# Second phase of a fused attention and expert kernel: rows turned on VectorE, last tile turned by halves, one layer moved ahead

## The chip, the cores and the metric

The kernel runs on one core of a Trainium2 chip. The metric is the device time of one execution in microseconds (us). Times inside the kernel are those of one profiled execution, counted from its first instruction. TensorE is called PE, its weight loads PEld, VectorE DVE, ScalarE ACT, GpSimd POOL and SyncE SP, as in the profile.

## What is computed

Three stages run one behind the other, all in float32:

```python
kv = einsum('bhsd,bhse->bhde', k, v); out = einsum('bhsd,bhde->bhse', q, kv)   # 8 x 8 heads, 576 x 64
x = out / sqrt(mean(out * out) + 1e-6) * g_norm                                # 4608 tokens of 512
h = x @ w_in; x = (max(h, 0) + alpha * min(h, 0)) @ w_out                      # 512 -> 2048 -> 512
logits = x @ w_gate + modality_bias[modality_id]; e = argmax(logits)           # 8 experts
y = gate * (max(x @ w1[e], 0) @ w2[e])                                         # 512 -> 1024 -> 512
```

## The kernel before, in words

**Precision.** A float32 operand of a large product is split into a high part (hi, cast to the type that PE takes, on ACT) and a remainder (lo, subtracted on DVE or POOL). Each product is then three matmuls: hi by hi, hi by lo, lo by hi.

**First phase.** Twelve chunks of 384 tokens (NCH = 12). For each chunk sixteen steps s: `first(c, s)` makes a block of 128 hidden rows, DVE applies the activation, ACT casts it (ghi, L377), POOL makes glo (L379), and `second(c, s - 1)` adds the block before into three PSUM tiles y (L393). While a chunk runs, the chunk before it gets its eight gate products (`dots`, L410, one per token tile and expert, on DVE), its choice of expert (`choose`, `count` on PE at L456 and L457, `place`) and is scattered by expert into the DRAM buffer `xb`. For the last chunk these follow in the second phase: the copies of y out of PSUM (`y_out`, L404, on ACT), sixteen or fewer of the gate products on DVE, ten on POOL and ACT (`far_mul`, L414, and `far_add`, L419).

**Second phase.** Tiles of 128 rows of `xb`, 41 in any case (MAIN) and up to 43. The experts' weights are loaded into two slots of `W`, each in two halves, by SP (`load_expert`, L593). The expert with most tokens ("leader") is known before the last chunk is through, so tiles 0 to 3 (EARLY = 4) are its rows and start while the last chunk is still being sorted; for later tiles PE reads from a table which slot to use (`words`, L1000).

For each tile i:
- `load_rows(i)`: four DMAs into `xs[:, i % 3]` and one of 8 B per row (`tail`). For tiles 0 to 2 (PLAIN = 3) the pieces are 32 numbers long (128 B), for the others 128 numbers (512 B). SP issues tiles 0 to 5, POOL the rest.
- `turn_rows(i)`: makes the transposed hi and lo in `xhi` and `xlo`, the buffers that hold the chunk's x in the first phase. Tiles 0 to 2: four PE transposes into PSUM (L631), a copy (L643), a subtraction (L644). Later tiles: one DVE transpose of 32 x 32 blocks (L647), a copy that puts the blocks in order (L649), a subtraction (L650).
- `layer1(i)`: 24 matmuls into `pair`, two halves of 512 columns, each with twelve; then the ReLU into `hh`. Tiles 0 to 2 and tile 40: two whole copies on ACT (L687). Others: sixteen quarters of 32 x 256, eight on DVE and eight on ACT, which also move blocks (L692).
- `turn_h(i)`: the transposed hi and lo of `hh` (`hth`, `htl`): with PE transposes (L631, L706, L707) for tiles 0 to 2 and tile 40, else on DVE and ACT (L709, L712, L713), half by half.
- `layer2(i)`: 24 matmuls into one PSUM tile, a scaled copy on ACT (L730), a scatter into the output by POOL (L732).

**Order.** The program order is written out by hand, and every engine works through its own queue in that order. The ends of the first phase and the start of the second are, for PE: `first(11, 15)`, `second(11, 14)`, turn of tile 0's rows, `second(11, 15)`, turn of tile 1's rows, `layer1(0)`, turn of tile 2's rows, the first half of `layer1(1)`, `turn_h(0)`, its second half, `layer2(0)`, the count, `turn_h(1)`, `layer1(2)`, `layer2(1)` with `turn_h(2)` inside, and then the loop (L993): for i = 3 to 40 `turn_rows(i + 1)`, `layer1(i)`, `layer2(i - 1)`, `turn_h(i)`; at last `layer2(40)`. SP's queue at that place is: rows of tile 0, first half of the leader's weights, rows of tiles 1 and 2, second half of the weights (L938 to L942); `layer2(0)` reads the second half.

Of the kernel before, what the change touches and what calls it, by code (L numbers as in the profile page):

```python
# [8 lines left out]
F32 = mybir.dt.float32  # L9
F32R = mybir.dt.float32r  # L10
# [12 lines left out]
D = 512  # L23
# [15 lines left out]
NTAB = 48  # L39
FAR = [(1, e) for e in range(E)] + [(2, 6), (2, 7)]  # L40
PLAIN = 3
EARLY = 4
DOTS = (0, 2, 5, 8, 11, 14, 17, 20, 22, 24)
LAST_DOTS = (0, 3, 6, 9, 12, 15, 18, 21, 24)
# [3 lines left out]
def fused(ctx: ExitStack, tc, qT, kv, g2, wmoe, alpha, wgate, bias, modality, w12, out):  # L48
# [58 lines left out]
    def other(n=512):  # L107
        return (pools[1] if pools else ps_a).tile([128, n], F32, tag="a", name="a")
# [498 lines left out]
    def load_rows(i):  # L607


        if i >= NIT:  # L610
            return
        tab = tab_0[0:1, 1 + i:2 + i] if i < EARLY else tab_row[0:1, i:i + 1]
        q = SP if i < 6 else G
        r = q.value_load(tab, min_val=0, max_val=E * BUCKET + 1024 - 128)
        rows[i] = four(xs[:, i % 3, :])
        src = xb[ds(r, 128)]
        for b in range(4):
            if i < PLAIN:
                to, of = rows[i][:, b].rearrange("p (r i) -> p r i", r=4), src[:, 0:D].rearrange("p (r c i) -> p c r i", r=4, c=4)[:, b]
            else:  # L620
                to, of = rows[i][32 * b:32 * b + 32], src[:, 128 * b:128 * b + 128].rearrange("(a j) c -> j a c", j=32)
            d = q.dma_start(to, of)
        row_dma[:] = [d.ins.name]
        q.dma_start(tail[:, i, :], src[:, D:D + 2])

    order = lambda t: t.rearrange("p (c a j) -> p c a j", c=4, a=4)

    def turned(x, to=None):
        ps = ps_y.tile([128, D], F32, tag="y", name="turned") if pools else to
        for k in range(4):  # L630
            PE.transpose(ps[:, k * 128:(k + 1) * 128], x[:, k * 128:(k + 1) * 128], ident)  # L631
        return ps

    def turn_rows(i):

        x = rows.pop(i)
        o = (i % 3) * 512
        hi = xhi.rearrange("p a b -> p (a b)")[:, o:o + 512]
        lo = xlo.rearrange("p a b -> p (a b)")[:, o:o + 512]
        flat = x.rearrange("p a b -> p (a b)")  # L640
        if i < PLAIN:
            ps = turned(flat, None if pools else spare if i else other())
            A.copy(hi, ps)  # L643
            V.tensor_tensor(lo, ps, hi.bitcast(F32), ALU.subtract)  # L644
            x2[i] = hi, lo
            return
        V.transpose(flat, flat)  # L647
        x = x.rearrange("p a (c j) -> p c a j", c=4)
        A.copy(order(hi), x)  # L649
        V.tensor_tensor(order(lo), x, order(hi).bitcast(F32), ALU.subtract)  # L650
        x2[i] = hi, lo

    def mm(i, ps, a, o, start, stop):
        w = (W if i < EARLY else regs[i][0])[:, o:o + 512]
# [6 lines left out]
    def layer1(i, between=None):  # L661
        if i >= EARLY:
            j, slot = PE.alloc_register(f"j{i}"), PE.alloc_register(f"slot{i}")
            PE.reg_alu(j, words[i // 8], 3 * (i % 8), ALU.logical_shift_right)
            PE.reg_alu(j, j, 7, ALU.bitwise_and)
            PE.reg_alu(slot, j, 1, ALU.bitwise_and)
            PE.reg_alu(slot, slot, SLOT, ALU.mult)
            j, slot = PE.snap(j, min_val=0, max_val=7), PE.snap(slot, min_val=0, max_val=SLOT)
            regs[i] = W[:, ds(slot, SLOT)], j * 2 + 2
            PE.wait_ge(sem_w, j * 2 + 1)  # L670
        hi, lo = x2.pop(i)
        pair = pools[0].tile([128, 2, 512], F32, tag="h", name="h2")
        h = one.tile([128, 2, 512], F32, tag="qT", name="hh")
        for n in range(2):
            ps = pair[:, n, :]
            for k in range(4):
                o = (k * 2 + n) * 1024
                a, b = hi[:, k * 128:(k + 1) * 128], lo[:, k * 128:(k + 1) * 128]
                mm(i, ps, a, o, k == 0, False)
                mm(i, ps, a, o + 512, False, False)  # L680
                mm(i, ps, b, o, False, k == 3)
            if n == 0 and between:
                between()

        plain = i < PLAIN or i == MAIN - 1
        for n in range(2 if plain else 0):
            A.activation(h[:, n].rearrange("p (c b i) -> p b c i", b=4, c=4), pair[:, n].rearrange("p (b c i) -> p b c i", b=4, c=4), AF.Relu)  # L687
        for a in range(0 if plain else 4):
            for b in range(4):
                to, of = h[32 * b:32 * b + 32, :, 128 * a:128 * a + 128], pair[32 * a:32 * a + 32, :, 128 * b:128 * b + 128]  # L690
# [5 lines left out]
        A.sem_inc(sem_1, 1)  # L696
        hh[i] = h

    def turn_h(i):
        h = hh.pop(i)  # L700
        hi = pools[2].tile([128, 2, 512], F32R, tag="kv", name="hth")
        lo = two.tile([128, 2, 512], F32R, tag="raw", name="htl", bufs=3)
        for n in range(2):
            if i < PLAIN or i == MAIN - 1:
                ps = turned(h[:, n])
                A.copy(hi[:, n], ps)  # L706
                V.tensor_tensor(lo[:, n], ps, hi[:, n].bitcast(F32), ALU.subtract)  # L707
                continue
            V.transpose(h[:, n], h[:, n])  # L709
            u, v = order(hi[:, n]), order(lo[:, n])  # L710
            x = h[:, n].rearrange("p (a c j) -> p c a j", c=4, a=4)
            A.copy(u, x)  # L712
            V.tensor_tensor(v, x, u.bitcast(F32), ALU.subtract)  # L713
        ht[i] = (t.rearrange("p n (c t) -> p (n c) t", t=128) for t in (hi, lo))

    def layer2(i, between=None):
        if i >= EARLY:
# [48 lines left out]
    with tc.manual_schedule():  # L766
# [77 lines left out]
        for c in range(NCH):  # L844
# [3 lines left out]
            for s in range(NFB):  # L848
                edge = s == NFB - 1
                between = None  # L850
                if edge and nxt < NCH:
                    between = lambda: [take_x(nxt, k) for k in range(2)]
                elif s == 0 and c > 0:
                    between = lambda: [second(c - 1, NFB - 1, (2,)), y_out(c - 1, 1), y_out(c - 1, 0)]
                if c == 0:
# [21 lines left out]
                if edge and nxt < NCH:  # L877
                    for k in range(2, 4):
                        take_x(nxt, k)
                    second(c, s, (0, 1))  # L880
                elif edge:
                    turn_rows(0)
                    second(c, s)

                if kvb and s in (3, 7):
                    kv_mm(kvb[0], s - 3 and 2)
# [65 lines left out]
        c = NCH - 1  # L952
        y_out(c, 1)
        y_out(c, 2)
        turn_rows(1)
        phase1.close()
        pools.append(ctx.enter_context(tc.tile_pool(name="ps_p", bufs=2, space=PSUM)))
        pools.append(ctx.enter_context(tc.tile_pool(name="ps_o", bufs=1, space=PSUM)))
# [5 lines left out]
        dots(c, 16, 22)  # L964
        layer1(0, lambda: add(0, 1, 2, 3))
        y_out(c, 0)
        turn_rows(2)
        load_rows(3)
        dots(c, 0, 2)
        add(4, 5)  # L970
# [19 lines left out]
        for j in range(1, E):  # L990
            load_expert(j)
        layer2(1, lambda: turn_h(2))
        for i in range(PLAIN, MAIN):  # L993
            if i + 1 < MAIN:
                turn_rows(i + 1)
            layer1(i)
            if i < MAIN - 3:
                load_rows(i + 3)
            if i == PLAIN:
                _, words[:] = nc.values_load_multi_w_load_instructions(  # L1000
                    tab_pe[0:1, 0:6], engines=[PE.engine], min_val=0, max_val=8 ** 8 - 1)
            if i == 8:
                items = nc.values_load(tab_pe[0:1, 6:7], min_val=0, max_val=NIT)
            layer2(i - 1)
            turn_h(i)
        layer2(MAIN - 1)
        with tc.If(items > MAIN):
            for i in range(MAIN, NIT):
# [49 lines left out]
```

## Time and profile before

| | |
|---|---|
| Median of 3 runs | 1359.06 us (1358.51 to 1362.18) |
| Profiled execution | 1360.58 us, its span 1358.9 us, granted PE clock 0.997 |
| PE busy | 1340.9 us (99% of the span) |
| PE weight loads busy | 1155.2 us (85%) |
| DVE, ACT, POOL busy | 987.8, 526.4, 669.5 us (73%, 39%, 49%) |
| DMA | 250.69 MB, 184 GB/s on average |
| Second phase | from `layer1(0)` at 889.93 us to the end |

A row of the timeline gives the start in us, the duration in us, the engine, the line of the program, the operation, the tile written and the tiles read, a count where equal neighbours are merged, and in square brackets how long the engine had been idle and what the profile names as the releaser. An engine's name with a q is its instruction queue, where DMAs are issued and registers loaded. Matmuls overlap in PE's pipeline, so the distance of two starts is the pace, not the duration.

### The profile page before, as it was taken

The numbers are of one execution on the slowest core, as the hardware profiler recorded it, in microseconds if no ns is written. First come the engines' busy times: TensorE is split into PE (matmuls) and PEld (weight loads), VectorE is DVE, ScalarE is ACT, GpSimd is POOL, SyncE is SP. The second block draws the span as 40 slices with busy tenths as digits, with TensorE's granted clock in tenths as the row PEclk, the third lists the DMA queues.
The fourth block names the chain that finished last, engine by engine and source line by source line (L and its number), as shares of the span: only waits on it lengthen the run. The fifth ranks groups of instructions, "written<-read, shape, count | busy, mean of one in ns | idle before, by whom it ended". The sixth has DMA issues, their size and how long they took to land. (4 is left out here: it accounts for less than half of the span.)

```text
span 1358.9 us, 26721 instructions
## 1 busy us (share of the span) xinstructions
PE 1340.9 (99%) x8886; PEld 1155.2 (85%) x8886; DVE 987.8 (73%) x2204; ACT 526.4 (39%) x1147; POOL 669.5 (49%) x643
## 2 busy tenths in 40 slices
PE   8999999999999999999999999999999999999997
PEld 7878888888888988988888988878888888888886
DVE  5778777787877787968787878666766666666662
ACT  3873233332323323232323333144555544445442
POOL 2866555565655564746464656453333333333320
PEclk8999999999999999999999999999999999999999
DMA  7956646453546463546554443557411171637784
GB/s 257 320 191 210 217 145 201 165 200 131 185 163 212 153 221 117 201 160 221 175 191 171 140 164 117 184 204 243 177 48 48 58 281 47 269 106 298 305 322 162
DMA packets 88949, 250.69 MB, mean 184 GB/s; under 512 B 19245, under 2 KB 39213, under 8 KB 86640
## 3 DMA queue, kind: packets, MB, share of 16 engines
q1 hardware_dynamic: 77056, 220.82, 46.2%
q0 software_dynamic: 11760, 28.14, 6.3%
q8 instruction: 78, 1.28, 0.4%
q14 instruction: 55, 0.45, 0.1%
HBM read 158.69 MB, written 91.54 MB: 184 GB/s over the span
## 5 line engine op out<-in xcount | busy, mean ns | idle before, releaser
L365 PE MATMUL h<-xhi,W 128*128 128x384 f32 x1536 | 429.7, 341 | 0.5 <-POOL W L183 0.2
L379 POOL TENSOR_TENSOR glo<-gg,ghi 128x384 fp32r<-128x384 f32 x192 | 234.7, 1223 | 340.1 <-ACT ghi L377 324.4
L393 PE MATMUL y<-W,ghi 128*128 128x512 f32 x1152 | 299.1, 394 | 4.8 <-ACT ghi L377 3.7
L377 ACT CAST ghi<-gg 128x384 fp32r<-128x384 f32 x192 | 98.8, 515 | 501.1 <-DVE gg L373 232.6
L365 PEld LDWEIGHTS h<-xhi,W 128*128 128x128 f32 x1536 | 280.4, 188 | 11.2 <-ACT xhi L354 1.2
L365 PE MATMUL h<-xlo,W 128*128 128x384 f32 x768 | 257.9, 336 | 0.0
L393 PEld LDWEIGHTS y<-W,ghi 128*128 128x128 f32 x1152 | 213.0, 188 | 44.6 <-ACT ghi L377 8.7
L410 DVE CUSTOM_DVE_ANT_0 junk<-yrow,wg_sb 128x512 f32<-128x512 f32 x242 | 221.0, 913 | 8.7 <-ACT yrow L404 3.1
L655 PE MATMUL h<-W,xhi 128*128 (+1 forms) x656 | 206.5, 396 | 0.0
L655 PE MATMUL y<-W,hth 128*128 (+1 forms) x656 | 204.6, 393 | 1.9 <-DVE lg L410 1.5
L213 POOL TENSOR_TENSOR raw<-raw 128x512 f32<-128x512 f32 x128 | 203.3, 1588 | 0.0
L372 DVE TENSOR_SCALAR gg<-h,alpha_sb 128x384 f32<-128x384 f32 x176 | 108.2, 615 | 106.3 <-PE h L365 104.2
L732 POOL DMA_INDIRECT out_dram<-kvbd,tail x41 | 43.2, 1054 | 282.8 <-ACT kvbd L730 239.6
L393 PE MATMUL y<-W,glo 128*128 128x512 f32 x576 | 163.4, 392 | 0.0
L365 PEld LDWEIGHTS h<-xlo,W 128*128 128x128 f32 x768 | 144.3, 188 | 6.0 <-DVE xlo L355 0.2
L655 PEld LDWEIGHTS h<-W,xhi 128*128 128x128 f32 x656 | 122.6, 187 | 29.9 <-ACT xhi L649 0.3
L655 PEld LDWEIGHTS y<-W,hth 128*128 128x128 f32 x656 | 123.0, 188 | 28.9 <-DVE lg L410 1.9
L655 PE MATMUL h<-W,xlo 128*128 (+1 forms) x328 | 129.4, 394 | 0.0
L393 PEld LDWEIGHTS y<-W,glo 128*128 128x128 f32 x576 | 107.9, 188 | 23.4 <-POOL glo L379 0.8
L655 PE MATMUL y<-W,htl 128*128 (+1 forms) x328 | 127.8, 390 | 0.0
L692 DVE TENSOR_SCALAR hh<-h 32x256 f32<-32x256 f32 x296 | 123.2, 416 | 4.6
L713 DVE TENSOR_TENSOR htl<-hh,hth 128x512 fp32r<-128x512 f32 x74 | 51.2, 692 | 99.0 <-ACT hth L712 97.6
(221 smaller groups left out, 1482.1 us busy)
## 6 DMA issues: line engine op xcount, KB each, us to landing
wsp<-raw SPq DMA_DIRECT2D x128, 512.0 KB
W<-wsp SPq DMA_DIRECT2D x16, 4096.0 KB
raw<-in_w_dram SPq DMA_DIRECT2D x128, 256.0 KB
kvt<-in_kv_dram SPq DMA_DIRECT2D x30, 512.0 KB
xs<-xb POOLq DMA_DIRECT2D x140, 64.0 KB
raw<-in_wmoe_dram SPq DMA_DIRECT2D x17, 511.8 KB
qT<-in_qT_dram SPq DMA_DIRECT2D x11, 768.0 KB
wg_sb<-in_wmoe_dram SPq DMA_DIRECT2D x15, 511.8 KB
```

What stands on the lines that cost most here:

```text
L213: G.tensor_tensor(lo, lo, hi, ALU.subtract)
L365: PE.matmul(ps, w_at(fb, part)[:, k * 128:(k + 1) * 128], x[:, k, :], start=(i == 0), stop=(i == 11))
L372: V.tensor_scalar(gg, ps, 0.0, alpha_sb[:, fb:fb + 1], ALU.min, ALU.mult)
L377: A.copy(ghi, gg)
L379: G.tensor_tensor(glo, gg, ghi.bitcast(F32), ALU.subtract)
L393: PE.matmul(y_t[c][t], a[:, t * 128:(t + 1) * 128], w, start=(fb == i == 0), stop=(fb == NFB - 1 and i == 2))
L410: V.tensor_tensor_reduce(spare if i >= 22 else junk, y, wg_sb[:, e, :], 1.0, 0.0, ALU.mult, ALU.add, lg_t[c][:, t, e:e + 1])
L655: m = PE.matmul(ps, a, w, start=start, stop=stop)
L692: m = V.tensor_scalar(to, of, 0.0, None, ALU.max) if mine else A.activation(to, of, AF.Relu)
L713: V.tensor_tensor(v, x, u.bitcast(F32), ALU.subtract)
L732: d = G.indirect_dma_start(out=out, out_offset=IndirectOffsetOnAxis(ap=tail[:, i, 1:2].bitcast(I32), axis=0), in_=y, in_offset=None, bound ...
```

## The change

- Tiles 0 to 2: their rows are loaded in the 512 B pieces, and turned like those of the later tiles, with a DVE transpose. The steps are written into the last two steps of the first phase: the DVE transpose of tile 0 at the end of step 14, its hi inside `first(11, 15)`, its lo and all of tiles 1 and 2 in step 15, ahead of `second(11, 15)` in the program and of the copies `y_out(11, 1)` and `y_out(11, 2)`.
- Tiles 3 and 40 (SPLIT): the ReLU is done per half of `pair` in quarters of 32 x 128. The first half's quarters, its transpose and its hi are written between the two halves of `layer1`, the rest behind it; tile 40 is no longer turned on PE.
- `layer2(3)` comes directly behind `layer2(2)`, ahead of `layer1(4)`; `turn_rows(4)` is written inside it, and the table's words are loaded behind it. From tile 4 on the loop is as before, with `layer2(4)` behind `layer1(5)`.

```diff
+SPLIT = (PLAIN, MAIN - 1)
 ...
         for b in range(4):
-            if i < PLAIN:
-                to, of = rows[i][:, b].rearrange("p (r i) -> p r i", r=4), src[:, 0:D].rearrange("p (r c i) -> p c r i", r=4, c=4)[:, b]
-            else:
-                to, of = rows[i][32 * b:32 * b + 32], src[:, 128 * b:128 * b + 128].rearrange("(a j) c -> j a c", j=32)
-            d = q.dma_start(to, of)
+            d = q.dma_start(rows[i][32 * b:32 * b + 32], src[:, 128 * b:128 * b + 128].rearrange("(a j) c -> j a c", j=32))
...
+    def turn_blocks(i):
+        flat = rows[i].rearrange("p a b -> p (a b)")
+        V.transpose(flat, flat)
+
+    def take_rows(i, part):
+        hi, lo = (order(t.rearrange("p a b -> p (a b)")[:, (i % 3) * 512:(i % 3) * 512 + 512]) for t in (xhi, xlo))
+        x = rows[i].rearrange("p a (c j) -> p c a j", c=4)
+        if part == 0:
+            A.copy(hi, x)
+            return
+        V.tensor_tensor(lo, x, hi.bitcast(F32), ALU.subtract)
+        rows.pop(i)
...
     def turn_rows(i):
...
-        if i < PLAIN:
-            ps = turned(flat, None if pools else spare if i else other())
-            A.copy(hi, ps)
-            V.tensor_tensor(lo, ps, hi.bitcast(F32), ALU.subtract)
-            x2[i] = hi, lo
-            return
...
+        turn_blocks(i)
+        take_rows(i, 0)
+        take_rows(i, 1)
...
             if n == 0 and between:
                 between()
-
-        plain = i < PLAIN or i == MAIN - 1
+            if n == 0 and i in SPLIT:
+                quarters(i, pair, h, slice(0, 1))
+                half_hi(i, h, 0)
+
+        plain = i < PLAIN
...
+        if not plain:
+            quarters(i, pair, h, slice(i in SPLIT, 2))
+        A.sem_inc(sem_1, 1)
+        hh[i] = h
+        if i in SPLIT:
+            half_lo(i, h, 0)
+            half_hi(i, h, 1)
+            half_lo(i, h, 1)
+            parts(i)
...
+                elif edge:
+                    between = lambda: take_rows(0, 0)
...
                 elif edge:
-                    turn_rows(0)
+                    take_rows(0, 1)
+                    turn_blocks(1)
+                    take_rows(1, 0)
+                    turn_blocks(2)
+                    take_rows(2, 0)
+                    take_rows(1, 1)
+                    take_rows(2, 1)
                     second(c, s)
+
+                if nxt == NCH and s == NFB - 2:
+                    turn_blocks(0)
...
-        turn_rows(1)
...
-        turn_rows(2)
...
         layer2(1, lambda: turn_h(2))
-        for i in range(PLAIN, MAIN):
+        layer1(3)
+        load_rows(6)
+        layer2(2)
+        layer2(3, lambda: turn_rows(4))
+        _, words[:] = nc.values_load_multi_w_load_instructions(
+            tab_pe[0:1, 0:6], engines=[PE.engine], min_val=0, max_val=8 ** 8 - 1)
+        for i in range(EARLY, MAIN):
...
-            layer2(i - 1)
-            turn_h(i)
+            if i > EARLY:
+                layer2(i - 1)
+            if i not in SPLIT:
+                turn_h(i)
         layer2(MAIN - 1)
```

`quarters`, `half_hi`, `half_lo` and `parts` hold the operations that stood in `layer1` and `turn_h` before, for one half: sixteen quarters; a DVE transpose and an ACT copy; a DVE subtraction.

## Rows read from the trace of the kernel before

**Rows 1.** Part 1 of the page: busy time, share of the span, instructions.
```profile
PE 1340.9 (99%) x8886; PEld 1155.2 (85%) x8886; DVE 987.8 (73%) x2204; ACT 526.4 (39%) x1147; POOL 669.5 (49%) x643
```

**Rows 2.** Timeline of PE from 886 to 910 us, in part.
```profile
887.06 0.60 PE L631 MATMUL a<-ident,xs 128*128 128x128 f32 x4
887.41 1.64 PE L393 MATMUL y<-W,ghi 128*128 128x512 f32 x6
...
902.27 0.39 PE L655 MATMUL h<-W,xlo 128*128 128x512 f32 x1
904.18 0.71 PE L655 MATMUL y<-W,hth 128*128 128x512 f32 x2 [1.52 <-DVE lg L410]
...
909.77 0.19 PE L456 MATMUL a<-hb,tri 128*128 128x24 bf16 x1
```

**Rows 3.** Timeline of SP's queue: DMA issues, from tile 1's rows on.
```profile
875.37 9.18 SPq L622 DMA_DIRECT2D xs<-xb  x4
...
888.46 2.07 SPq L622 DMA_DIRECT2D xs<-xb  x4
...
891.93 0.35 SPq L593 DMA_DIRECT2D W<-wsp  x1
...
928.18 1.95 SPq L622 DMA_DIRECT2D xs<-xb  x4
```

**Rows 4.** DMA view of 874.2 to 886, 884.8 to 886 and 904.5 to 910 us.
```profile
DMA packets 669, 4.27 MB, mean 362 GB/s; under 512 B 540, under 2 KB 540, under 8 KB 540
...
DMA packets 358, 0.11 MB, mean 91 GB/s; under 512 B 356, under 2 KB 356, under 8 KB 356
...
q1 hardware_dynamic: 720, 0.26, 22.6%
```

**Rows 5.** Timeline of ACT, POOL and DVE from 886 to 907 us, in part.
```profile
886.58 0.51 ACT L377 CAST ghi<-gg 128x384 fp32r<-128x384 f32 x1 [3.65 <-DVE gg L373]
889.55 1.07 ACT L404 COPY yrow<-y 128x512 f32<-128x512 f32 x2 [1.27 <-PE y L393]
890.21 7.60 POOL L414 TENSOR_TENSOR kvbd<-yrow,wg_sb 128x512 f32<-128x512 f32 x6 [2.03 <-ACT yrow L404]
895.98 1.06 ACT L687 ACTIVATE hh<-h 128x512 f32<-128x512 f32 x2
899.46 1.08 ACT L706 CAST hth<-turned 128x512 fp32r<-128x512 f32 x2 [0.22 <-PE turned L631]
907.04 0.18 DVE L437 CAST hb<-hot 128x24 bf16<-128x24 f32 x1
```

**Rows 6.** One line's instructions: durations in ns (least, median, most).
```profile
L712 ACT CAST hth<-hh x74: 607/619/622, 938.7 to 1336.4; 128x512 fp32r<-128x512 f32 x74
L692 DVE TENSOR_SCALAR hh<-h x296: 404/416/421, 934.4 to 1331.7; 32x256 f32<-32x256 f32 x148
```

**Rows 7.** Timeline of PE and DVE from 922 to 940 us, in part.
```profile
922.71 0.63 PE L655 MATMUL h<-W,xhi 128*128 128x512 f32 x2
...
928.30 0.62 PE L655 MATMUL y<-W,hth 128*128 128x512 f32 x2
...
932.42 0.71 DVE L647 STREAM_TRANSPOSE xs<-xs 128x512 f32<-128x512 f32 x1 [7.35 <-DMA xs<-xb]
...
933.84 0.73 PE L655 MATMUL h<-W,xhi 128*128 x2
...
939.80 0.62 PE L655 MATMUL y<-W,hth 128*128 128x512 f32 x2
```

**Rows 8.** Line 1000: the load of the table's words on PE's sequencer.
```profile
L1000 PEldq TENSOR_LOAD <-tab_pe x1: 1018/1018/1018, 924.1 to 924.1; - x1
```

**Rows 9.** Timeline of DVE and PE from 1337 us on, in part.
```profile
1337.02 0.69 DVE L713 TENSOR_TENSOR htl<-hh,hth 128x512 fp32r<-128x512 f32 x1 [0.69 <-ACT hth L712]
...
1344.68 1.03 PE L631 MATMUL turned<-ident,hh 128*128 128x128 f32 x8
...
1351.75 0.40 PE L655 MATMUL y<-W,htl 128*128 x1
```

More of the change, by code (lines that the diff above doesn't have):

```diff
@@ L626, in fused, with turned @@
     order = lambda t: t.rearrange("p (c a j) -> p c a j", c=4, a=4)
-    def turned(x, to=None):
-        ps = ps_y.tile([128, D], F32, tag="y", name="turned") if pools else to
+    def turned(x):
+        ps = ps_y.tile([128, D], F32, tag="y", name="turned")
         for k in range(4):
@@ L632, in turned @@
         return ps
-    def turn_rows(i):
[L636 to L640, printed above, removed]
-        if i < PLAIN:
-            ps = turned(flat, None if pools else spare if i else other())
-            A.copy(hi, ps)
-            V.tensor_tensor(lo, ps, hi.bitcast(F32), ALU.subtract)
-            x2[i] = hi, lo
-            return
[L647 to L651, printed above, removed]
+    def turn_blocks(i):
[9 more added lines that the diff above has]
+        rows.pop(i)
+        x2[i] = (t.rearrange("p a b -> p (a b)")[:, (i % 3) * 512:(i % 3) * 512 + 512] for t in (xhi, xlo))
+    def turn_rows(i):
+        turn_blocks(i)
+        take_rows(i, 0)
+        take_rows(i, 1)
     def mm(i, ps, a, o, start, stop):
@@ L683, in layer1, with quarters @@
                 between()
-        plain = i < PLAIN or i == MAIN - 1
+            if n == 0 and i in SPLIT:
+                quarters(i, pair, h, slice(0, 1))
+                half_hi(i, h, 0)
+        plain = i < PLAIN
         for n in range(2 if plain else 0):
             A.activation(h[:, n].rearrange("p (c b i) -> p b c i", b=4, c=4), pair[:, n].rearrange("p (b c i) -> p b c i", b=4, c=4), AF.Relu)
-        for a in range(0 if plain else 4):
+        if not plain:
[7 more added lines that the diff above has]
+            parts(i)
+    def quarters(i, pair, h, ns):
+        for a in range(4):
             for b in range(4):
-                to, of = h[32 * b:32 * b + 32, :, 128 * a:128 * a + 128], pair[32 * a:32 * a + 32, :, 128 * b:128 * b + 128]
+                to, of = h[32 * b:32 * b + 32, ns, 128 * a:128 * a + 128], pair[32 * a:32 * a + 32, ns, 128 * b:128 * b + 128]
                 mine = a < 2
@@ L695, in layer1, with halves, half_hi, half_lo @@
                 tc.add_to_no_dep_group(f"quarters{mine}", m.ins)
-        A.sem_inc(sem_1, 1)
-        hh[i] = h
+    def halves(i):
+        if i not in ht:
+            ht[i] = (pools[2].tile([128, 2, 512], F32R, tag="kv", name="hth"),
+                     two.tile([128, 2, 512], F32R, tag="raw", name="htl", bufs=3))
+        return ht[i]
+    def half_hi(i, h, n):
+        hi, _ = halves(i)
+        if i < PLAIN:
+            of = turned(h[:, n])
+            A.copy(hi[:, n], of)
+            return of
+        V.transpose(h[:, n], h[:, n])
+        A.copy(order(hi[:, n]), h[:, n].rearrange("p (a c j) -> p c a j", c=4, a=4))
+    def half_lo(i, h, n, of=None):
+        hi, lo = halves(i)
+        if i < PLAIN:
+            V.tensor_tensor(lo[:, n], of, hi[:, n].bitcast(F32), ALU.subtract)
+            return
+        V.tensor_tensor(order(lo[:, n]), h[:, n].rearrange("p (a c j) -> p c a j", c=4, a=4), order(hi[:, n]).bitcast(F32), ALU.subtract)
+    def parts(i):
+        ht[i] = tuple(t.rearrange("p n (c t) -> p (n c) t", t=128) for t in halves(i))
     def turn_h(i):
         h = hh.pop(i)
-        hi = pools[2].tile([128, 2, 512], F32R, tag="kv", name="hth")
-        lo = two.tile([128, 2, 512], F32R, tag="raw", name="htl", bufs=3)
         for n in range(2):
[L704 to L714, printed above, removed]
+            half_lo(i, h, n, half_hi(i, h, n))
+        parts(i)
     def layer2(i, between=None):
@@ L998, in fused @@
                 load_rows(i + 3)
-            if i == PLAIN:
-                _, words[:] = nc.values_load_multi_w_load_instructions(
-                    tab_pe[0:1, 0:6], engines=[PE.engine], min_val=0, max_val=8 ** 8 - 1)
             if i == 8:
                 items = nc.values_load(tab_pe[0:1, 6:7], min_val=0, max_val=NIT)
-            layer2(i - 1)
-            turn_h(i)
+            if i > EARLY:
+                layer2(i - 1)
+            if i not in SPLIT:
+                turn_h(i)
         layer2(MAIN - 1)
```

## The prediction

> **What bounds the kernel now.** First the page: TensorE (PE) is busy for 99% of the span [rows 1], so only three things can pay: PE work that goes away, gaps in PE's row, and what ends those gaps. Then PE's row in the timeline, read for gaps between 885 us and the end. I number the second phase's tiles from 0; "hi" and "lo" are the two parts into which an operand is split, "turn" is the transpose. There are four places. (a) Three groups of four PE transposes turn the rows of tiles 0 to 2; one group stands here, the other two are alike [rows 2]. (b) The first matmul of layer2(0) starts at 904.18; the one before it started at 902.27 and the pitch is 0.23, so PE stands 1.68 us [rows 2]. The profile names a dot product of VectorE, but layer2(0) reads none of those; I read it as the second half of the leader's weights, issued at 891.93 [rows 3], which it does read. (c) Layer1(4) waits for the rows of tile 4, which VectorE turns when they land, at 932.42 [rows 7]. (d) At the end the eight transposes of tile 40 and the copies behind them stand alone between layer2(39) and layer2(40) [rows 9]. The rest of the second phase is one matmul per 0.23 us without a gap.
>
> **Part 1, rows of tiles 0 to 2 on VectorE.** Away go 3 x 4 PE transposes. Each group moves PE's next work by 887.41 - 887.06 = 0.35 us [rows 2], and the matmuls behind it lose another 0.07 to 0.1 in refilling (the first six take 1.64 where steady ones take 1.54), so 0.43 x 3 = 1.3 us. Against it: the last MoE product now follows at once on the one before it, at 887.06, and its operand ghi is written at 886.58 + 0.51 = 887.09 [rows 5]; its weight load, due 0.22 ahead, slips to about 887.15, which costs 0.2. PE gains 1.1 us by layer2(0).
>
> By the Trainium skill's page "TensorE: Matmul & The Clock Gate" (Part 4: PE-mode transpose) a transpose takes about 275 ns in a kernel's context; at that price the twelve here and the eight at the end would give 5.5 us. The rows show why that price does not add up: four last 0.60 together [rows 2], so they overlap, and the sum above goes by what follows them.
>
> The loads of these rows change too: the same four DMAs each, but in pieces of 512 B instead of 128 B, a quarter as many. On SP's queue they stand between the two halves of the leader's weights, order unchanged. Before, the four of tile 1 took 9.18 us to issue behind the first half, so tile 2's were issued only at 888.46 and the second half at 891.93 [rows 3]; layer2(0) could start 904.18 - 891.93 = 12.25 after that. After, I expect SP not to be held back, and all of them to lie in the queue when the first half ends. When is that? Its 129 large packets (669 less 540 small ones) go out within 874.2 to 886.0, eight on each of 16 engines, so about 1.3 us a packet, and only two start after 884.8 [rows 4]: most engines are through at some 885.9, the slowest near 887.2. A tile in 512 B pieces, its tail and semaphores take 22.6% of 5.5 us = 1.24 per engine (tile 3's) [rows 4]; two tiles 2.5. From landing to VectorE I put 0.5, at most 1.1 (tile 4 was turned at 932.42, 2.3 after its last issue ended, against 1.24 of data [rows 3, 7]). So tile 2 can be turned at **R** = 888.9 (engines alike) to 890.8 (the slowest, late landing); 0.3 less if SP gets through tile 0 sooner too. I take 889.5, between the two engine cases with the short landing (888.9 and 890.2). The second half then follows from 888.3 to 889.7 on instead of 892.2, and lands near 900 to 901.4. PE wants it at 902.5 - 1.1 = 901.4: the 1.68 goes, with at most 0.2 left.
>
> What is late next is the choice of experts for the last chunk. The count matmul, at 909.77 [rows 2], needs VectorE's hb, which is ready at 907.22 [rows 5]: 2.5 us of cover. By PE alone it would move to 909.77 - 1.1 - 1.68 = 907.0. But ACT and VectorE now wait for R ahead of the last chunk's work. On ACT tile 2's hi stands before the copies of y (L404). From R: turn 0.71 [rows 7], hi 0.62 [rows 6], so those copies start at R + 1.4 (before 889.55). First product on POOL 0.66 later, relu(0) behind four sums another 895.98 - 890.21 = 5.77 later, the copies of tile 0's turned h 2.8 after that (before 899.46 - 895.98 = 3.48, less 0.48 for tile 2's hi, now done, and 0.2 of waiting for PE), hb 907.22 - 899.46 = 7.76 later [rows 5]. Sum: R + 18.4. VectorE's own queue (turn, two lo, eight dot products) is ready sooner. So the count starts at the later of 907.0 and R + 18.4; with R = 889.5 at 907.9. **The head gains 909.77 - 907.9 = 1.9 us**; ends: R = 888.6 gives 2.8, R = 890.8 gives 0.6. From the count on (places, scatter, table, rows 3 to 5, with SP's and POOL's queues behind them) everything follows the count and shifts with it.
>
> Tile 0's turn lies on VectorE between the last two activations, where it waits for PE, and its hi on ACT before ghi, after the matmuls that read the old xhi: nothing.
>
> **Part 2, layer2(3) ahead of layer1(4).** The PE work is the same. Layer1(4) starts 5.5 us later, so the wait for tile 4's rows goes: layer1(4) took 939.80 - 933.84 = 6.0 where layer1(3) took 928.30 - 922.71 = 5.6 [rows 7], a gain of **0.4**. Layer2(3) wants tile 3 5.5 us after layer1(3). By halves: eight VectorE operations of 32x128 per half. Their price is not in the trace: 32x256 takes 0.42 [rows 6], 512 columns 0.69 [rows 9], so 1.08 ns a column and 0.28 for 128; the bounds are half of 0.42 and the whole. At 0.28 x 8 = 2.3 a half, first-half lo is ready 2 us early, at the upper bound just in time: nothing. Layer2(4) now follows layer1(5) directly, so tile 4 has 5.6 us for quarters (8 x 0.42 = 3.4), turn (0.7), hi (0.6) and lo (0.7) = 5.4 plus 0.3 of start; lo is wanted by the third matmul: a wait of 0.05, at most 0.2. The table's words are now loaded on PE's sequencer directly before their use: a load of 1.02 at 924.1 [rows 8] and register steps behind it, begun 4.2 us before the matmul that stood next in the order, at 928.30 [rows 7]; with that lead I cost it at nothing, at most 0.5. POOL's load of tile 7's rows moves behind one more output scatter; the rows are wanted two tiles later: nothing.
>
> **Part 3, tile 40 by halves.** Layer2(40) starts where the transposes did, at 1344.68 [rows 9]. At the pitch of layer2(2), 5.5 us for 24 matmuls [rows 7], its last one starts 5.27 later, at 1349.95 instead of 1351.75 [rows 9]: **1.8 us**. Cover: VectorE is free at 1337.02 + 0.69 = 1337.71 [rows 9]; quarters 2.3, turn 0.7, quarters 2.3, lo 0.7 end at 1343.7 where 1345.1 will do; turn, hi and lo of the second half at 1345.8 where 1347.4 will do. At 0.42 a quarter the first lo comes at 1346.0: 0.9 of the gain would go.
>
> **Sum.** 1.9 + 0.4 - 0.05 + 1.8 = 4.05 us. The profiled execution took 1360.58 (span 1358.9 and 1.7 around it), 1.5 over the median of the runs, 1359.06; the gaps are no part of that difference that I can see, so I take the sum off the median: **1355.0 us**.
>
> **Rivals.** *Tile 2 late as before.* SP is still held behind the weights, and tile 2 is issued near 888.5 and there at 892.1. Speaks for it: the four issues of tile 1 that were held (9.18) [rows 3], with nothing in the trace that shows 512 B pieces behind weights. Against: a quarter of the pieces. Then count at 910.5, the head loses 0.7, the sum is 1.4 or a little less: 1357.8. *R early.* No slow engine, R at 888.6 or below, PE itself sets the count: 2.8 + 2.15 = 4.95: 1354.1. *PE waits for the first halves.* Tiles 3 and 40 now read one half of the pair in PSUM while PE writes the other. If that held PE until the first half's quarters are done, tile 3 would cost 2.5, tile 40 (VectorE free at 1337.71, the half done at 1344.68 - 5.5 - 2.8 = 1336.4) 3.6, together 6.1: 1361.1, slower. It turns slower where the two waits pass 4.05. No operation of the trace reads one half beside writes into the other; against it speaks that the halves are separate 512-column regions. The Trainium skill's page "PSUM — Partial Sum Buffer" (PSUM bank collisions raise a hardware error) wants readers and TensorE on different banks, and counts 512 FP32 values to a bank; no run here shows it.
>
> **How the numbers follow.** Forecast 0.45, R early 0.18, tile 2 late 0.25, PE waits 0.05, something unseen 0.07. Range: from 1353.7 (R early, less the spread of the median) to 1358.3 (tile 2 late, with a bit of part 3 lost). A measurement of this kernel tells about 0.3%, 4.1 us, from no change: below 1355.0 is faster. The forecast sits on that line: half of it and most of R early make 0.38 for faster; 0.58 within; 0.04 slower.
>
> **What would show it.** Right: no transposes of xs on PE; layer2(0) without a gap; SP's five issues of tile 1 in about 2.5 us; ACT's copies of y at 890 to 891.5 and the count right behind hb; layer1(4) without a gap; layer2(40) straight behind layer2(39). Wrong: tile 2's DMAs still issued after 888, relu(0) or hb later than here with PE waiting for them, or a gap of PE between the halves of layer1(3) and layer1(40).

## The result, and the profile after

The changed kernel takes **1366.57 us** (median of six executions, 1363.32 to 1369.89); the kernel before took 1359.13 beside it. The ratio is 1.0051, interval 1.0033 to 1.0069: about 7 us slower, where the prediction said 4 us faster. The page of one execution of 1363.32 us (span 1361.7), part 1, which answers to [rows 1]:

```profile
PE 1337.8 (98%) x8866; PEld 1152.0 (85%) x8866; DVE 996.6 (73%) x2233; ACT 531.5 (39%) x1169; POOL 669.6 (49%) x643
```

PE has 20 instructions less (the transposes), is busy for 3 us less, and yet the span is longer: the time has gone into PE's gaps. The view of what PE waits for, from 880 us to the end, is short (engine and line, what it waited for, us in total, times, longest):

```profile
PE h L652 <- DVE hh L703: 6.3, 2, 3.8
PE turned L628 <- ACT hh L687: 1.5, 1, 1.5
PE y L652 <- DMA W<-wsp: 0.2, 1, 0.2
```

Lines are those of the changed kernel: L652 the matmuls of both layers, L703 the quarters, L687 the relu of tiles 0 to 2, L628 the turn of h on PE, L394 the last MoE products, L457 the count, L438 hb, L619 the loads of rows, L594 those of weights, L633 the turn of rows on VectorE, L639 and L641 their hi and lo, L720 and L721 the turn and the hi of h, L405 the copies of y, L415 POOL's products, L753 the scaling of a result. In the kernels of the experiments lines behind L652 can stand up to four further down. PE's timeline in part (start, duration, engine, line, operation; in brackets the idle time before it and its releaser), with VectorE's first quarters of tile 3; it answers to [rows 2, 7, 9]:

```profile
882.32 1.54 PE L394 MATMUL y<-W,ghi 128*128 128x512 f32 x6
...
896.68 1.15 PE L628 MATMUL turned<-ident,hh 128*128 128x128 f32 x8 [1.49 <-ACT hh L687]
...
900.86 0.71 PE L652 MATMUL y<-W,hth 128*128 128x512 f32 x2 [0.23 <-DMA W<-wsp]
906.53 0.17 PE L457 MATMUL a<-hb,tri 128*128 128x24 bf16 x1
...
919.46 0.63 PE L652 MATMUL h<-W,xhi 128*128 128x512 f32 x2
...
922.03 0.39 PE L652 MATMUL h<-W,xlo 128*128 128x512 f32 x1
922.45 2.36 DVE L703 TENSOR_SCALAR hh<-h 32x128 f32<-32x128 f32 x8 [0.29 <-PE h L652]
924.96 0.70 PE L652 MATMUL h<-W,xhi 128*128 128x512 f32 x2 [2.54 <-DVE hh L703]
...
927.81 0.62 PE L652 MATMUL y<-W,hth 128*128 128x512 f32 x2
...
955.50 0.63 PE L652 MATMUL h<-W,xhi 128*128 x2
...
1335.24 0.39 PE L652 MATMUL h<-W,xlo 128*128 x1
1339.40 0.79 PE L652 MATMUL h<-W,xhi 128*128 x2 [3.77 <-DVE hh L703]
...
1340.42 1.05 PE L652 MATMUL h<-W,xhi 128*128 x2
...
1343.81 0.63 PE L652 MATMUL y<-W,hth 128*128 x2
...
1354.58 0.40 PE L652 MATMUL y<-W,htl 128*128 x1
```

Layer1(3) and layer1(40) stop in the middle: twelve matmuls into the first half of the pair, then nothing until the first half's quarters have been read, then twelve into the second. Behind tile 40's stop the matmuls are also slow: two take 1.05 where two took 0.63. The page gives the granted clock of such a stretch (stretch, its length, PE's busy time and instructions, granted clock in the fourth number, DMA share, GB/s), after first, then before:

```profile
10.00:15.00 5.00, 4.61 (x34) 1.00 1.08 355
...
1340.00:1345.00 5.00, 5.00 (x17) 0.67 0.11 43
```
```profile
5.00:10.00 5.00, 2.64 (x15) 0.90 0.80 236
10.00:15.00 5.00, 5.00 (x22) 0.50 1.10 334
15.00:20.00 5.00, 5.00 (x36) 0.92 1.02 388
```

So for part of 1340 to 1345 PE ran at 1.2 GHz, the lower level. The second fence warns of something else: the profiled execution of before spent some 7 us of its startup at the lower level, that of after did not; the first MoE matmul starts at 27.10 before and at 24.31 after, and the last MoE product but one, ahead of all that the change touches on PE, at 884.99 and 882.32, 2.67 earlier. Of the twelve profiled executions of this study six have a granted clock of 0.66 or less from 10 to 15 us and four one of 0.67 to 0.76 near 100 us (one of them both), whatever the kernel. Absolute times of two profiles can't be subtracted here; distances from a common mark in PE's row can. Three marks of before that are not shown yet:

```profile
884.99 1.54 PE L393 MATMUL y<-W,ghi 128*128 128x512 f32 x6
...
956.42 0.63 PE L655 MATMUL h<-W,xhi 128*128 x2
...
1339.18 0.62 PE L655 MATMUL y<-W,hth 128*128 x2
```

| from ... to (us) | before | after | change | forecast |
|---|---|---|---|---|
| last MoE product but one ... count | 24.78 | 24.21 | -0.57 | -1.9 |
| count ... layer1(3) | 12.94 | 12.93 | -0.01 | 0 |
| layer1(3) ... layer1(6) | 33.71 | 36.04 | +2.33 | -0.35 |
| layer1(6) ... last matmul | 395.33 | 399.08 | +3.75 | -1.8 |
| **all** | 466.76 | 472.26 | **+5.5** | -4.05 |

The third line holds tile 3's stop, 2.76 (2.70 of standing, from 922.03 + 0.23 to 924.96, and 0.06 of slower first matmuls behind it), less 0.43 by which layer1(4), now without a gap, is shorter. The fourth holds tile 40's stop (1335.24 + 0.23 to 1339.40, 3.93), the slow matmuls behind it (twelve in 4.41 where twelve took 2.8, 1.6) and the gain of the tail, 1.80: layer2(39) to the last matmul takes 10.77 where it took 12.57.

### The profile page after: what moved, and what is told of

It is laid out like the page before. It is cut to its first block, busy times and chain, and to the rows that moved or that the text cites. A ratio compares the mean times of both kernels' runs of the same rounds, so it can differ in the third digit from the quotient of the medians.

```text
span 1361.7 us, 26738 instructions
## 1 busy us (share of the span) xinstructions
PE 1337.8 (98%) x8866; PEld 1152.0 (85%) x8866; DVE 996.6 (73%) x2233; ACT 531.5 (39%) x1169; POOL 669.6 (49%) x643
## 5 line engine op out<-in xcount | busy, mean ns | idle before, releaser
L394 PE MATMUL y<-W,ghi 128*128 128x512 f32 x1152 | 299.1, 394 | 4.8 <-ACT ghi L378 3.8
L394 PEld LDWEIGHTS y<-W,ghi 128*128 128x128 f32 x1152 | 213.0, 188 | 44.9 <-ACT ghi L378 9.3
L652 PE MATMUL h<-W,xhi 128*128 (+1 forms) x656 | 207.5, 397 | 6.3 <-DVE hh L703 6.3
L652 PE MATMUL y<-W,hth 128*128 (+1 forms) x656 | 204.4, 393 | 0.2 <-DMA W<-wsp 0.2
L394 PE MATMUL y<-W,glo 128*128 128x512 f32 x576 | 163.4, 392 | 0.0
L652 PEld LDWEIGHTS h<-W,xhi 128*128 128x128 f32 x656 | 123.5, 189 | 37.2 <-ACT hh L703 7.1
L652 PEld LDWEIGHTS y<-W,hth 128*128 128x128 f32 x656 | 123.1, 188 | 27.1 <-DVE htl L726 0.6
L703 DVE TENSOR_SCALAR hh<-h 32x256 f32<-32x256 f32 (+1 forms) x320 | 129.0, 403 | 15.2 <-PE h L652 10.3
L652 PE MATMUL h<-W,xlo 128*128 (+1 forms) x328 | 129.9, 396 | 0.0
L703 ACT ACTIVATE hh<-h 32x256 f32<-32x256 f32 (+1 forms) x320 | 117.3, 367 | 30.5 <-PE h L652 26.4
L394 PEld LDWEIGHTS y<-W,glo 128*128 128x128 f32 x576 | 107.9, 188 | 23.5 <-POOL glo L380 0.8
L652 PE MATMUL y<-W,htl 128*128 (+1 forms) x328 | 127.7, 389 | 0.0
```

The lines of the kernel that those rows point to most:

```text
L652: m = PE.matmul(ps, a, w, start=start, stop=stop)
```

## The experiments

Theory: PE's stop is a wait written into the program, because the pair of halves is guarded as one piece; it costs the two gaps and, where the clock falls behind them, more. The rivals: reading one bank beside writing its neighbour is slow in itself; the halves were needed, and what lost was something else; the loss sits in the head.

**The wait taken away.** The two tiles' second-half matmuls are told apart from the first half's quarters; nothing else changes.

```diff
+                free = n == 1 and i in SPLIT
-                mm(i, ps, a, o, k == 0, False)
+                mm(i, ps, a, o, k == 0, False, free)
...
+        if free:
+            for mine in (True, False):
+                tc.declare_no_dep(m.ins, group=f"quarters{mine}", reason="they read the other bank of the pair")
```

> The changed kernel, but the second-half matmuls of layer1(3) and layer1(40) are no longer made to wait for the quarters that read the first half of the pair. My theory: PE's two stops are a wait written into the program for those quarters, and neither the data nor the memory needs it. Then both gaps (2.76 and 3.93 us) go, the half-clock stretch behind the second (about 1.6) with them, and what is left against the kernel before is the gain of the head 0.57, of layer1(4) 0.43 and of the tail 1.80: together 2.8 us faster, about 1356.3, ratio 0.998. Rival A: ACT and VectorE reading one bank while PE writes its neighbour slow each other, so that the time is lost anyway as slower matmuls or quarters: 2 to 6 us slower than before. Rival B: the loss is not in these gaps but in the head (tile 2's rows late): then it stays at 1.005.

Measured: **1357.33 us**, ratio 0.9983 (0.9974 to 0.9992). PE and VectorE in the middle of layer1(3), and the marks at the end:

```profile
924.28 0.40 PE L652 MATMUL h<-W,xlo 128*128 128x512 f32 x1
924.52 0.63 PE L652 MATMUL h<-W,xhi 128*128 128x512 f32 x2
...
924.72 2.37 DVE L707 TENSOR_SCALAR hh<-h 32x128 f32<-32x128 f32 x8 [0.56 <-PE h L652]
...
1337.78 0.62 PE L652 MATMUL y<-W,hth 128*128 x2
...
1348.54 0.39 PE L652 MATMUL y<-W,htl 128*128 x1
```

PE goes from one half to the next at its pitch of 0.23 while VectorE reads the first half, and the eight quarters take 2.37 as they did with PE standing (2.36): neither slows the other, and rival A is out. From mark to mark the changes against before are -0.33, +0.01, -0.42 and -1.80, together 2.5; the medians say 2.35. The theory holds, and the stretches of parts 2 and 3 are shorter by what the prediction gave them. The Trainium skill's page "PSUM — Partial Sum Buffer" (PSUM bank collisions raise a hardware error) asks for a guard bank by bank, and a half is one bank; the trace agrees that more is not needed.

**Tiles 3 and 40 in one piece.** No halves, so nothing to guard.

```diff
-SPLIT = (PLAIN, MAIN - 1)
+SPLIT = ()
...
         layer1(3)
+        turn_h(3)
```

> The changed kernel, but tiles 3 and 40 are turned on VectorE in one piece, behind both halves, as the other tiles are: no first half is read before the second is written, so no wait inside layer1. Quarters of 32x256 (8 x 0.42 = 3.4 us), turn 0.7, hi 0.6, lo 0.7 give 5.4 against the 5.5 us of a layer2. Theory (only the wait inside layer1 costs): both gaps are gone, at most 0.3 us is waited before layer2(3) and layer2(40): 2.3 to 2.8 us faster than before, 1356.5, ratio 0.998. Rival (the halves are needed because a whole tile is too late behind one layer2): more than 1 us lost before layer2(3) and again before layer2(40), so no faster than before.

Measured: 1359.42, ratio 0.9999 (0.9990 to 1.0008). That is the rival's time, but not for its reason: both stops are gone, and layer2(3) starts without a gap although its tile, too, has only the 5.5 us of one layer2 to be turned in; only layer2(40) is late. ACT's row and PE's in this kernel:

```profile
1344.49 0.69 ACT L753 ACTIVATE kvbd<-y,tail 128x512 f32<-128x512 f32 x1 [2.40 <-PE y L652]
1345.07 0.61 ACT L721 CAST hth<-hh 128x512 fp32r<-128x512 f32 x1
...
1345.73 0.74 PE L652 MATMUL y<-W,hth 128*128 x2 [1.28 <-ACT hth L721]
```

Tile 40's hi stands in ACT's queue behind the scaling of layer2(39)'s result, which waits for PE; its turned block was ready at 1343.24. So the order is at fault, not the length. From layer2(39) on this kernel takes 12.58, 1.8 more than without PE's wait, and ahead of layer1(4) another 0.44 goes, behind a gap of 0.22; together 2.3, where the ratios say 2.2. Its profiled execution also has a granted clock of 0.87 and 0.78 from 895 to 905 us, behind a wait of 1.82 ahead of the turn of tile 0's h, and with it a head of 25.51 us, 0.73 longer than before.

**The same, turned ahead of layer2(39).**

```diff
+            if i == MAIN - 1:
+                turn_h(i)
             if i > EARLY:
                 layer2(i - 1)
-            if i not in SPLIT:
+            if i < MAIN - 1:
                 turn_h(i)
```

> e2_whole (tiles 3 and 40 turned in one piece), and the turning of tile 40 is written ahead of layer2(39). In e2_whole PE waited 1.28 us before layer2(40), and ACT's row shows why: tile 40's hi stands behind the scaling of layer2(39)'s result, which waits for PE until 1344.49, while the turned block lay ready from 1343.24. Theory: with the order changed hi starts at 1343.2, hi and lo of the first half are there by 1344.5, PE waits at most 0.3 us instead of 1.28, and the kernel is 1.0 to 1.4 us faster than e2_whole against the same kernel before: ratio 0.9990 or a little less. So not the halves but their order in ACT's queue is what part 3 needs. Rival (the whole tile is simply too late behind 5.5 us of layer2): 0.9999 as e2_whole.

Measured: 1358.46, ratio 0.9989 (0.9980 to 0.9998). ACT in this kernel:

```profile
1344.08 0.62 ACT L721 CAST hth<-hh 128x512 fp32r<-128x512 f32 x1 [1.19 <-DVE hh L720]
...
1346.72 0.69 ACT L753 ACTIVATE kvbd<-y,tail 128x512 f32<-128x512 f32 x1
```

Hi now starts when the turned block is there, PE shows no gap ahead of layer2(40), and layer2(39) to the last matmul takes 10.79, as with the halves. By the ratios 1.4 us comes back; the two intervals just overlap, so it is the rows that show it. Part 3's gain needs no halves, so no wait: only that ACT's queue takes the turn before the scaling.

**Part 1 alone.** The changed kernel with tile 40 and the order of the layers put back as they were.

```diff
-SPLIT = (PLAIN, MAIN - 1)
+SPLIT = ()
...
-        plain = i < PLAIN
+        plain = i < PLAIN or i == MAIN - 1
...
-        layer1(3)
-        load_rows(6)
-        layer2(2)
-        layer2(3, lambda: turn_rows(4))
...
-        for i in range(EARLY, MAIN):
+        for i in range(PLAIN, MAIN):
```

> Part 1 alone: the rows of tiles 0 to 2 turned on VectorE, the order of layers 1 and 2 and the turning of tile 40 as before. Theory (from the profile of the changed kernel): SP is held at tile 2's rows, the copies of y stand on ACT behind tile 2's hi, and the count comes 0.57 us earlier than before: 0.6 faster, 1358.5, ratio 0.9996. My prediction on record said 1.9 (ratio 0.9986). Rival (the loss of the whole change sits in part 1, which only starts 2.7 us early by chance in the one profile): slower than before by 2 us or more.

Measured: 1358.63, ratio 0.9990 (0.9981 to 0.9999). From the mark to the count its profile has 24.16, 0.62 less than before. The head gains a third of its forecast and loses nothing. The same profile holds one thing more. VectorE turns tile 4's rows in it at

```profile
930.95 0.71 DVE L633 STREAM_TRANSPOSE xs<-xs 128x512 f32<-128x512 f32 x1 [5.46 <-DMA xs<-xb]
```

which is 45.25 us behind the mark (885.70) where it was 47.43 before (932.42 from 884.99 [rows 7]), and layer1(4) takes 5.59 where it took 5.96, though the layers stand in their old order. So part 1 alone already brings the 0.4 that was forecast for part 2.

**Without part 3.** Tile 40 turned on PE, tile 3 still by halves.

```diff
-SPLIT = (PLAIN, MAIN - 1)
+SPLIT = (PLAIN,)
...
-        plain = i < PLAIN
+        plain = i < PLAIN or i == MAIN - 1
```

> The changed kernel without part 3: tile 40 is turned on PE as before, tile 3 still by halves with PE's wait inside layer1(3). Theory: of the gaps only tile 3's 2.76 us stays: 2.76 - 0.57 - 0.43 = 1.8 us slower than before, 1360.8, ratio 1.0013. If the granted clock also falls behind tile 3's gap, another 1 to 3 us, and the matmuls behind that gap stand at twice the pitch. Rival (part 3 is no loss, all of it is tile 3 and the head): as slow as the changed kernel, 1.005.

Measured: 1363.20, ratio 1.0027 (1.0015 to 1.0038): 3.5 us slower. Its profile has tile 3's stop alone ([2.54], and 36.06 from layer1(3) to layer1(6)) and the full clock behind it: 2.35 more there, 0.39 less in the head, 2.0 together, as the theory has it. The other 1.5 I put down to the clock of other executions: three of the seven had a mean granted clock of 0.993 or 0.994, the median one 0.997, against 0.998 here. That is inferred, since only their mean clock is known; the next run shows such a stretch.

**The changed kernel once more.**

> The changed kernel unaltered, one more profiled execution. Six executions of it fall into two groups, mean granted clock 0.997 (1363.3 to 1365.7 us) and 0.993 (1367.4 to 1369.9). Theory: the granted clock falls for some microseconds behind PE's waits, always behind tile 40's 3.8 us and sometimes behind one of the shorter ones (1.5 us ahead of the turn of tile 0's h, 2.5 us inside layer1(3)); an execution of the second group shows a stretch at half clock behind one of these as well, some 3.7 us more. Rival: the second group is slow somewhere in the first phase, away from the change. In an execution of the first group only the stretch behind tile 40's gap shows.

Measured: one execution, 1368.67 us. PE inside layer1(3), and the granted clock of the stretches around it:

```profile
928.91 1.19 PE L652 MATMUL h<-W,xhi 128*128 128x512 f32 x2 [2.54 <-DVE hh L703]
...
930.33 1.05 PE L652 MATMUL h<-W,xhi 128*128 128x512 f32 x2
```
```profile
10.00:15.00 5.00, 4.52 (x18) 0.54 1.09 322
15.00:20.00 5.00, 5.00 (x31) 0.78 1.01 369
925.00:930.00 5.00, 2.46 (x9) 0.86 0.43 145
930.00:935.00 5.00, 5.00 (x19) 0.80 0.69 144
...
1345.00:1350.00 5.00, 5.00 (x16) 0.66 0.26 105
```

The same stop of 2.54 us, and this time the clock falls behind it: twelve matmuls in 4.26 where after took 2.85, 1.4 us more. Tile 40's stop is followed by the lower clock again. So the theory's stretch is there, but it is worth 1.4 and not 3.7. The larger part of this execution's distance to the first one, 3.75 us at the mark ahead of the change (886.07 against 882.32), is the startup's: 0.54 and 0.78 from 10 to 20 us, where after has the full clock. As to that part the rival was right.

**Why the head gained so little.** SP's queue, VectorE and ACT of the changed kernel, which answer to [rows 3, 5]:

```profile
872.63 1.94 SPq L619 DMA_DIRECT2D xs<-xb  x4
...
875.91 10.71 SPq L619 DMA_DIRECT2D xs<-xb  x4
...
888.02 0.36 SPq L594 DMA_DIRECT2D W<-wsp  x1
...
888.31 0.71 DVE L633 STREAM_TRANSPOSE xs<-xs 128x512 f32<-128x512 f32 x1 [0.93 <-DMA xs<-xb]
...
889.10 0.62 ACT L639 CAST xhi<-xs 128x512 fp32r<-128x512 f32 x1 [1.02 <-DVE xs L633]
889.62 1.07 ACT L405 COPY yrow<-y 128x512 f32<-128x512 f32 x2
```

Tile 1's issues are no longer held (1.94 where it was 9.18); tile 2's are (10.71), until the first half of the weights has landed. Two things follow: the second half is issued late, and tile 2's hi holds up the copies of y. Four kernels on top of the one without PE's wait take them up.

Tile 2's rows on POOL's queue:

```diff
-        q = SP if i < 6 else G
+        q = SP if i < 6 and i != 2 else G
```

> e1_nowait, and tile 2's rows are fetched on POOL's queue, not on SP's. Theory: in e1_nowait SP is held for 10.65 us at tile 2's rows until the first half of the leader's weights has landed (878.03 to 888.68), so the second half is issued at 890.07 and layer2(0) waits for it until 903.18; and the copies of y stand behind tile 2's hi, at 891.62. With tile 2 on POOL the second half is issued at about 878, lands some 3 us sooner, the 0.56 us before layer2(0) goes, tile 2 is there before tile 1, and the copies start about 0.9 earlier: the count moves by 1 to 1.5 us, so the kernel is 3.3 to 3.8 us faster than before, ratio 0.9974. Price: POOL's five issues took 3.5 us at tile 6, and its gap between two products here is 3.1 to 3.4, so PE may lose up to 1 us to a late product. Rival (SP's hold has no part in the count, the chain from the copies of y alone sets it): 0.9983 as e1_nowait, or 0.9977 by the 0.9 of the copies.

Measured: 1357.53, ratio 0.9983 (0.9974 to 0.9992). The second half is issued at 881.14, straight behind tile 1, and the wait ahead of layer2(0) is gone; tiles 1 and 2 are turned one straight behind the other, from 5.1 us behind the mark, so tile 2 at some 5.7 where it was 6.0, but tile 1 later than its 4.4. From the mark to the count 23.97, 0.48 less than without it: SP's hold had a part, less than expected, and the count now waits 0.31 for hb. The times don't show it.

Tile 2 turned behind the last copy of y, its rows fetched by SP as in after:

```diff
-                    turn_blocks(2)
-                    take_rows(2, 0)
                     take_rows(1, 1)
-                    take_rows(2, 1)
...
         y_out(c, 0)
+        turn_blocks(2)
+        take_rows(2, 0)
         load_rows(3)
         dots(c, 0, 2)
+        take_rows(2, 1)
```

> e1_nowait, and tile 2's rows are turned behind the last copy of y, where the kernel before had them, instead of ahead of the copies; the fetch stays on SP. The copies of y then start 1.5 us earlier (890.1 instead of 891.6) and relu(0) with them, so PE's wait of 1.49 us ahead of the turn of tile 0's h goes. Theory: the second half of the leader's weights lands no earlier than before, layer2(0) cannot start before 903.2, and the 1.5 us comes back as a wait there: 0.9983 as e1_nowait. Rival (the copies of y behind tile 2's hi are the whole cause of the head's missing gain): the count comes 1.3 us earlier, 0.9974.

Measured: 1356.42, ratio 0.9974 (0.9961 to 0.9986). PE in this kernel:

```profile
895.91 1.15 PE L628 MATMUL turned<-ident,hh 128*128 128x128 f32 x8 [0.36 <-ACT hh L691]
...
901.19 0.71 PE L652 MATMUL y<-W,hth 128*128 128x512 f32 x2 [1.33 <-DVE htl L730]
```

The wait moved as the theory says: 1.1 us less ahead of the turn of h, 0.8 more ahead of layer2(0), and 24.31 from the mark to the count, 0.14 less than without it. The ratio is nearer to the rival's, but its interval covers both, and no stretch of the profile from the mark on is shorter by 0.9; I count this as no gain shown. The profile names VectorE's lo of tile 0's h for the wait; the weights, issued at 888.85, come at about the same time, so the run doesn't tell which of the two was last.

Both edits together:

> e5_pool2 and e6_late2 together: weights early and copies of y not behind tile 2. Theory: both causes of the missing gain go; the copies start 1.5 us earlier than in e1_nowait, PE loses nothing ahead of the turn of tile 0's h nor ahead of layer2(0), and the count comes 1.5 to 2 us earlier unless VectorE's dot products, which now have the turn and the lo of tile 2 among them (1.4 us), end late: 0.8 to 2 us ahead of e1_nowait, so 3.1 to 4.3 faster than before, ratio 0.9973. That would be the 1.9 us that the prediction on record put on the head. Rival (VectorE's own queue sets the count): no better than e5_pool2.

Measured: 1357.97, ratio 0.9985 (0.9976 to 0.9994): the rival. PE waits 0.70 for the lo of tile 0's h and 0.67 for hb. VectorE and POOL show why:

```profile
900.00 1.70 DVE L641 TENSOR_TENSOR xlo<-xs,xhi 128x512 fp32r<-128x512 f32 x1
...
899.84 3.00 POOL L415 TENSOR_TENSOR kvbd<-yrow,wg_sb 128x512 f32<-128x512 f32 x2 [0.94 <-ACT kvbd L420]
```

Tile 2's lo takes 1.70 beside POOL's products where it takes 0.69 alone. So in the last kernel it is moved behind the choice:

```diff
         choose(c)
+        take_rows(2, 1)
         weigh(c)
```

> e7_both, and the lo of tile 2 is taken on VectorE behind the choice of experts instead of between the dot products. In e7_both that lo took 1.70 us beside a product of POOL, where the lo of tile 1, with POOL idle, took 0.69, and it stands in the chain of VectorE that ends in hb: the count waited 0.67 us for hb, and layer2(0) 0.70 us for the lo of tile 0's h. Theory: both waits go and the count comes about 1.4 us earlier than in e7_both, so the head finally gains 1.7 us on the kernel before and the whole is 3.5 to 4 us faster than before, ratio 0.9972. Rival (something else of the chain, ACT's sums or POOL's products, stands right behind hb): 0.9983 as the other versions without PE's wait.

Measured: 1356.76, ratio 0.9972 (0.9960 to 0.9983). VectorE and PE:

```profile
908.78 0.69 DVE L641 TENSOR_TENSOR xlo<-xs,xhi 128x512 fp32r<-128x512 f32 x1
...
908.92 0.17 PE L457 MATMUL a<-hb,tri 128*128 128x24 bf16 x1 [0.68 <-DVE hb L438]
```

The lo takes 0.69 again and the wait ahead of layer2(0) is gone, but the count still waits 0.68 for hb: from the mark 23.87, so the head gains 0.91, not 1.7. VectorE had 0.79 us to spare for ACT's copies of tile 0's h, and 1.93 for ACT's last copy of y; the chain through ACT, which begins with tile 1's hi (at 890.95, behind a turn at 890.16 for which VectorE had waited 3.03 us for the rows), sets the end by these rows. By its ratio this is the best version, 3.8 us under the kernel before (from the mark on its profile is 3.15 shorter); its interval overlaps that of the version that only loses PE's wait.

## Why the prediction was wrong

**The step that failed is the overlap inside layer1(3) and layer1(40).** The forecast's sum let the first half's quarters run beside the second half's matmuls and put PE's wait for them at nothing; in its place PE stood for 2.70 and 3.93. The prediction had this as its third rival, with the mechanism, the places and the price (2.5 and 3.6), and gave it 0.05, on the ground that the halves are separate, though no operation of the trace reads one half beside writes into the other. The halves are separate for the hardware; for the program they were not. Rows of the kernel before that the prediction does not use bear on that. ACT at the end of layer1(1), then ACT and PE around the end of layer1(2):

```profile
902.76 1.08 ACT L687 ACTIVATE hh<-h 128x512 f32<-128x512 f32 x2 [0.72 <-PE h L655]
...
916.52 1.09 ACT L687 ACTIVATE hh<-h 128x512 f32<-128x512 f32 x2 [4.91 <-issue]
...
916.10 0.39 PE L655 MATMUL h<-W,xlo 128*128 128x512 f32 x1
```

The relu is two operations, one for each half. For tile 1 the profile names PE as what ACT waited for, and the first relu starts 0.1 behind the end of the second half's last matmul (902.27 + 0.39 [rows 2]), though the first half's had ended at 898.98 and ACT stood idle. For tile 2 it names no releaser ("issue"): ACT had been idle for 4.91 us, the first half's matmuls had started their last at 913.30 and handed over to the second half at 913.53, and yet the first relu starts only when the last matmul of the second half has ended. By these rows readers of the pair are guarded against the pair, not against their half. From them the stop was the likelier case, and the rival's own 1361.1 would have been the forecast, with the right sign. That the guard is the cause, and not the hardware, is shown by the run without it; that it comes from the tile being tracked as one piece is what these rows suggest.

**The clock was not costed.** Where PE stops its clock may fall: tile 40's stop cost 3.93, and 1.6 more in both profiles of the changed kernel; tile 3's 2.76, and in one of the two 1.4 more. The stops were 0.6 longer than priced, the clock took 1.6 to 3.0, the head fell short by 1.3: 3.5 to 4.9 of the 5.5 by which the median lies above the rival's 1361.1. The rest, 0.6 to 2.0, stays open.

**Part 1** was mis-sized: 0.33 to 0.62 in the versions that contain it alone or without PE's stop, 0.57 in after, for 1.9; in the profiles of the two kernels with tiles in one piece, whose clock fell in the head, it is a loss of 0.73 and 0.91. The formula was right: R + 18.4 with the measured R, 888.31 + 2.67 = 890.98 on the clock of before, is 909.4, and the count came at 906.53 + 2.67 = 909.20. R was wrong: 889.5 was taken, 890.8 was the late end, because SP was expected not to be held. That held issues were moved from tile 1 to tile 2 and not removed is the rival "tile 2 late" in milder form. The kernels that undo this (0.81 and 0.91) show that even a free SP would not have brought 1.9: tile 1's rows land behind the first half's packets too, and its hi stands ahead of the copies.

**Part 2** came out in size, layer1(4) without a gap, 0.43 and 0.42 for 0.4; but part 1 alone brings the same, so no run shows what the new order is worth by itself. Eight quarters of a half took 2.36 for 2.3. The table's load cost nothing in after and without PE's wait, where it began 4.1 us ahead of layer1(4). In the two kernels with tiles in one piece it began only 3.1 ahead of that place, and PE shows a gap of 0.22 and 0.26 there, which cost 0.44; the profile names no releaser, so that it is the load is inferred. **Part 3's** tail was right: 1.80 for 1.8.

Without the stop the parts give 0.33 + 0.42 + 1.80 = 2.55; the sum on record, 4.05, is that and the 1.5 of the head.

## What to carry to other kernels

Before an engine is set to read one part of a buffer while another engine writes the rest, look in the trace of before for what guards that buffer: if a reader of one part waits for the end of both, the writer may wait for readers in the same way, as here, and the overlap becomes a stop. Price a stop of PE by the matmuls behind it as well as by its length. And where two profiles are compared, measure from a mark behind the startup; here the startup alone differed by as much as the change was worth.

## What the runs showed of the hardware

The granted clock fell behind PE's stops of 3.77 us in two of two profiles, behind 2.54 in one of three, behind 1.82 and 1.96 (the two kernels with tiles in one piece, ahead of the turn of tile 0's h) in two of two, and behind 1.25 to 1.58, at the same place, in none of six. In PE's row a fall cost 1.4 to 1.6 us each time.

SP's issues were held behind the 4 MB load at tile 1 with pieces of 128 B and at tile 2 with pieces of 512 B; with only two tiles in its queue it was not held at all (second half issued at 877.91 in the kernel with both changes).

VectorE's lo took 1.68 and 1.70 us beside POOL's products and 0.65 to 0.69 without. Both its operands lie in SBUF; the lo of h beside POOL, with one operand in PSUM, took 0.64 each. The Trainium skill's page "SBUF — State Buffer" (SBUF: two separate sides) says that a VectorE operation with two SBUF inputs and a POOL operation that reads SBUF block each other for a whole instruction; these rows agree with it.
